# Turning the exponentials of one key block on VectorE and by DMA instead of on TensorE

## The chip, the cores and the metric

The kernel runs on one core of one Trainium2 chip. The metric is the device time of one execution in microseconds (us): the median of three runs of the kernel before was 794.5 us (793.51 to 794.91). Engines are named as the profile names them: PE is TensorE (PEld its weight loads), DVE is VectorE, ACT is ScalarE, POOL is GpSimd, SP is SyncE, which here only issues DMA transfers.

## The reference, cut to what matters

```python
# q, k, v: (8 batches, 8 heads, 576 tokens, 64);  f: (8, 8, 576)
scores = scale * q @ k.T                       # 576 x 576 for each head
cum    = cumsum(log(clip(f, 1e-4, 1)))
scores = where(causal, -1e9, scores + cum[:, :, :, None] - cum[:, :, None, :])
attn   = softmax(scores)
x      = (attn @ v) as (8, 576, 512)
h = relu(x @ w_in); u, v = halves of h         # 512 -> 1024
v_n = layernorm(v); v_s = w_spatial @ v_n + b_spatial
out = (u * v_s) @ w_out
```

## The kernel before, in words

The 64 heads are worked on as 32 **pairs** P of two heads h, four pairs to a batch (`PPB` = 4). The 576 tokens of a head are four query blocks i of 128 and a tail of 64; keys come in the same blocks c. For a pair, `scores(P)` makes q k^T on PE for each query block i and the keys 0 to 128(i+1)-1 (L322), in two pieces: blocks 0, 1, 2 and then block 3. DVE adds the decay and takes the row minimum of the negated scores (L302), ACT takes the exponential and its row sum (L333), DVE forms 1/sum (L348, L349), and POOL scales the rows by it (`share`, L310; for pairs 5 to 7 ACT does, L308). The result lies in `tt[h]` with queries on the partitions. The product with v needs keys on the partitions, so `transposes(P, h)` (L421) turns it: for each key block c one PE transpose for each query block i >= c (L402), 4 + 3 + 2 + 1 of them, into a PSUM bank `tp`, and one copy from there into the tile `e` (L393), in turn by ACT and DVE. `scores_tail` and `transposes_tail` do the same for the 64 queries of the tail. `attend` (L431) then multiplies the blocks of `e` with v (L440) into two PSUM banks, both heads side by side. ACT rounds the sum to `xh` (L449), DVE forms the rest `xl` (L452), and with that the two banks are free for the next scores. `e` has two buffers, one for even and one for odd pairs.

`moe(b)` is the feed-forward part of batch b, nearly all PE matmuls of one pass (L229), its four stages cut into groups that accumulate in two PSUM banks `ps`; its output tile `o` is copied by ACT (L780) and sent to memory by a transfer that SP issues (L782).

The first four pairs run in `first()`, whose order is fixed as written. After that `attention(b)` and `moe(b)` run interleaved: at each `yield` a step says how much PE time it took, and the loop at the end takes next whatever is behind, by the totals `t_attn` and `t_moe`. In the steady state moe(b) thus runs beside the attention of batch b+1. The order in which the rows then stand on every engine's queue is set by a scheduler that runs over the written program at build time; each engine works its queue in order. For pair P, `attention` writes: transposes(P), scores(P+1), transposes_tail(P), scores_tail(P+1), product(P). SP's queue holds, for each pair, the loads of the decay rows `dk` and `dt` (L248, L250), of `qk_t` (L236) and of `vraw` (L287), and between them the outputs `o`.

Of the kernel before, what the change touches and what calls it, by code (L numbers as in the profile page):

```python
# [22 lines left out]
NB = 4  # L23
TL = 512
DM = 512
TOFF = (0, 128, 384, 768)
HALVES = ((0, 256), (256, 320))
QK = 640 + S
EOFF = (0, 640, 1280, 1088, 576)
# [7 lines left out]
def attn_gmlp_kernel(ctx: ExitStack, tc: tile.TileContext, qk, v, f, w_in, w_sp, b_sp, w_out, out):  # L37
# [34 lines left out]
    def decay_rows():  # L72
        ft = wk.tile([64, S], F32, name="ft", tag="vraw")
        SY.dma_start(out=ft, in_=f)
        yield
        ones = wk.tile([64, S], F32, name="ones", tag="xl", bufs=6)
        V.memset(ones, 1.0)
        cum = wk.tile([64, S], F32, name="cum", tag="xh", bufs=6)
        rt = cst.tile([64, RW], F32, name="rt", tag="e1")
        V.tensor_scalar(out=ft, in0=ft, scalar1=1.0e-4, scalar2=1.0, op0=ALU.max, op1=ALU.min)  # L80
        A.activation(ft, ft, AF.Ln)
        A.activation(lnc[0:1, 2:3], ft[0:1, 0:1], AF.Exp)
        V.tensor_tensor_scan(out=cum, data0=ones, data1=ft, initial=0.0, op0=ALU.mult, op1=ALU.add)
# [94 lines left out]
        load64(w_v[:, r, c, :], dh[:, r, c], dl[:, r, c], raw, w[:], t[:], mark)  # L178


    tt = [cst.tile([128, 1280], F32, name=f"tt{h}") for h in range(2)]
    tl = cst.tile([128, 640], F32, name="tl")
    G.memset(tl[:, S:640], 0.0)
    own = {}
# [86 lines left out]
    def mask(P, part=None):  # L271
# [9 lines left out]
        for p in (slice(0, 64), slice(64, 128)) if part != 0 else ():  # L281
            G.affine_select(out=dt[p, TL:S], in_=dt[p, TL:S], compare_op=ALU.is_ge, fill=-8.0 * BIG, base=0,
                            pattern=[[-1, 64]], channel_multiplier=1)

    def prep_v(P):
# [41 lines left out]
    def weigh(P, i, h, tt, dk, at, nm, sm):  # L327

        ps, c, m = at[i, h]
        n = 128 * (i + 1)  # L330
        t = tt[:, TOFF[i]:TOFF[i] + n]
        freed[m] = lowest(t, ps[:, c:c + n], decay(dk, i), nm)
        last["exp", P, h, i] = A.activation(t, t, AF.Exp, bias=nm, scale=-1.0, accum_out=sm)  # L333

    def scores(P):

        qk_t, dk, _ = tab[P]
        tt, _ = turn(P)
        nm = [wk.tile([128, 4], F32, name="nm", tag="nm", bufs=6) for h in range(2)]
        sm = [wk.tile([128, 4], F32, name="sm", tag="sm", bufs=6) for h in range(2)]  # L340
        for piece in ((0, 1, 2), (3,)):
            at = score_piece(P, qk_t, piece)
            yield 250 + 1.68 * 128 * sum(i + 1 for i in piece)
            for i in reversed(piece):
                for h in range(2):
                    weigh(P, i, h, tt[h], dk[h], at, nm[h][:, i:i + 1], sm[h][:, i:i + 1])
        for h in range(2):
            V.tensor_scalar(out=sm[h], in0=sm[h], scalar1=1.0e-9, scalar2=None, op0=ALU.add)  # L348
            V.reciprocal(sm[h], sm[h])  # L349
            for i in range(NB):  # L350
                n = 128 * (i + 1)
                t = tt[h][:, TOFF[i]:TOFF[i] + n]
                share(P, t, sm[h][:, i:i + 1])
        yield 0

    def scores_tail(P):
# [22 lines left out]
            mm(warm[0], zm[:, 0:128], zm[:, 0:512], True, True)  # L379

    nev = [0]
    es = {}

    def e_tile(P):
        if P not in es:
            es[P] = cst.tile([128, 2, 1600], F32, name="e", tag=f"e{P % 2}")
        return es[P]

    copied = {}

# [5 lines left out]
    def turn_block(P, h, c):  # L396
# [3 lines left out]
        tp = bank(2 + c, False) if P < PPB and c > 1 else PS['t'].tile([128, 512], F32, name="tp")  # L400
        for i in range(c, NB):
            T.transpose(out=tp[:, (i - c) * 128:(i - c + 1) * 128],  # L402
                        in_=tt[h][:, TOFF[i] + 128 * c:TOFF[i] + 128 * c + 128], identity=ident)
# [16 lines left out]

    def transposes(P, h):  # L421
        for c in range(NB):
            turn_block(P, h, c)()
            yield 107 * (NB - c)

    def transposes_tail(P):
        for cs, off, step in TAILS:
# [2 lines left out]

    def attend(P, xh, xl):  # L431

        vt, e = vts[P], es.pop(P)
        xb = 4 if P < PPB else 0
        x0, x1 = bank(xb), bank(xb + 1)
        jobs = []
# [1 line left out]
        def product(x, s0, q0, q1, c, h, end):  # L438
            e0 = EOFF[c] - 128 * c
            return lambda: T.matmul(x[64 * h:64 * h + 64, q0 - s0:q1 - s0], vt[:, c, h, :],  # L440
                                    e[:, h, e0 + q0:e0 + q1], start=c == 0, stop=c == end)

        for c in range(NB + 1):
            for x, s0, q0, q1, end in ((x1, 256, max(256, 128 * c), S, NB), (x0, 0, 128 * c, 256, 1)):
                jobs += [product(x, s0, q0, q1, c, h, end) for h in range(2) if c <= end]
        in_one_piece(jobs, copied.pop(P))
        yield 2950
        for ps, s0, n in ((x0, 0, 256), (x1, 256, 320)):
# [16 lines left out]
    def first(ws):  # L465
# [22 lines left out]
        def period(P):  # L488
# [14 lines left out]

            def spread(i, s_, by_a=False):
                for h in range(2):
                    t = tt[h][:, TOFF[i]:TOFF[i] + 128 * (i + 1)]
                    share(PPB + 1 if by_a else 0, t, s_[:, h, 0:1])

            def turned(h):
# [345 lines left out]
```

## Time and profile before

| | |
|---|---|
| median of three runs | 794.5 us |
| the profiled execution, its own time | 796.76 us |
| its span, first to last instruction | 794.8 us |
| PE busy | 759.3 us (96%) |
| DVE, ACT, POOL busy | 436.1 (55%), 418.9 (53%), 368.9 us (46%) |
| granted clock, mean | 0.990 |

All stage times below are on the profiled execution's span, which is 2.0 us shorter than that execution's own time; that time in turn is 2.3 us above the median of the three runs. A busy share is an average over the stages: the views by stretch say which engine is full where.

### The profile page before, as it was taken

The numbers are of one execution on the slowest core, as the hardware profiler recorded it, in microseconds if no ns is written. First come the engines' busy times: TensorE is split into PE (matmuls) and PEld (weight loads), VectorE is DVE, ScalarE is ACT, GpSimd is POOL, SyncE is SP. The second block draws the span as 40 slices with busy tenths as digits, with TensorE's granted clock in tenths as the row PEclk, the third lists the DMA queues.
The fourth block names the chain that finished last, engine by engine and source line by source line (L and its number), as shares of the span: only waits on it lengthen the run. The fifth ranks groups of instructions, "written<-read, shape, count | busy, mean of one in ns | idle before, by whom it ended". The sixth has DMA issues, their size and how long they took to land.

```text
span 794.8 us, 14578 instructions
## 1 busy us (share of the span) xinstructions
PE 759.3 (96%) x4924; PEld 604.5 (76%) x4925; DVE 436.1 (55%) x1509; ACT 418.9 (53%) x1134; POOL 368.9 (46%) x682
## 2 busy tenths in 40 slices
PE   8777898799999999999999999999999999999997
PEld 4445676587887778887788878877788877888896
DVE  6886998645644455444654446445654546543322
ACT  7855587745554456544654446454664446543331
POOL 3976664425544344453732456443544436432231
PEclk9999999899999999999999999999999999999999
DMA  7855254213333213343222243323132342200001
GB/s 218 233 169 160 73 147 155 67 58 123 97 97 123 89 51 95 98 123 122 82 96 67 74 137 97 96 101 103 62 87 89 123 135 81 66 30 31 28 1 67
DMA packets 34316, 78.48 MB, mean 99 GB/s; under 512 B 4161, under 2 KB 8257, under 8 KB 34242
## 3 DMA queue, kind: packets, MB, share of 16 engines
q1 hardware_dynamic: 33922, 77.03, 31.3%
q8 instruction: 39, 0.64, 0.3%
q10 hardware_dynamic: 320, 0.52, 0.2%
q14 instruction: 35, 0.29, 0.1%
HBM read 67.78 MB, written 9.75 MB: 98 GB/s over the span
## 4 chain that ended last, share of the span: by engine, by line
PE 70%; issue 5%; ACT 2%; DMA 2%; POOL 2%; DVE 1%; POOLq 0%; ACTq 0%; DVEq 0%; SPq 0%
PE ps L229 39%; PE sc L440 9%; PE tp L402 8%; PE sc L322 7%; PE sc L229 5%; PE tp L229 2%; DMA out_dram<-o 1%; POOL gl L756 1%; ACT tt L333 1%; PE tp L412 1%; POOL tt L310 1%; DMA dt<-rows_d 1%; DVE tt L302 1%; ACT gh L755 1%; ACT tt L308 0%
## 5 line engine op out<-in xcount | busy, mean ns | idle before, releaser
L333 ACT ACTIVATE tt<-tt,nm 128x128 f32<-128x128 f32 (+2 forms) x240 | 133.7, 558 | 101.5 <-DVE nm L302 99.7
L310 POOL TENSOR_SCALAR tt<-tt,sm 128x128 f32<-128x128 f32 x192 | 100.2, 541 | 109.8 <-DVE sm L349 109.7
L756 POOL TENSOR_TENSOR gl<-u,gh 128x256 fp32r<-128x256 f32 (+1 forms) x64 | 51.5, 806 | 142.4 <-ACT gh L755 141.7
L402 PE MATMUL tp<-ident,tt 128*128 128x128 f32 x588 | 109.4, 283 | 7.8 <-DVE e L393 4.5
L402 PEld LDWEIGHTS tp<-ident,tt 128*128 128x128 f32 x588 | 73.4, 141 | 44.8 <-issue 10.9
L440 PE MATMUL sc<-e,vraw 128*64 128x320 f32 (+4 forms) x896 | 96.8, 368 | 5.8 <-ACT tl L578 4.6
L302 DVE CUSTOM_DVE_ANT_1 tt<-sc,dk 128x256 f32<-128x256 f32 (+1 forms) x120 | 65.8, 552 | 57.5 <-PE sc L322 45.6
L440 PEld LDWEIGHTS sc<-e,vraw 128*64 128x64 f32 x896 | 61.9, 140 | 42.7 <-issue 11.0
L322 PE MATMUL sc<-qk_t 64*128 64x128 f32 (+3 forms) x512 | 87.7, 462 | 3.1 <-DVE nm L302 2.1
L393 DVE COPY e<-tp 128x384 f32<-128x384 f32 (+2 forms) x156 | 69.8, 450 | 26.2 <-PE tp L402 17.9
L393 ACT COPY e<-tp 128x256 f32<-128x256 f32 (+1 forms) x148 | 67.9, 459 | 27.5 <-PE tp L402 24.4
L229 PE MATMUL ps<-sph,vnh 128*128 128x256 f32 (+1 forms) x240 | 75.7, 315 | 1.0 <-DVE u L752 0.7
L229 PE MATMUL ps<-xh,winh 128*128 128x256 f32 (+1 forms) x232 | 74.5, 321 | 1.0 <-DVE vx L701 0.6
L229 PE MATMUL ps<-spl,vnh 128*128 128x256 f32 (+1 forms) x240 | 71.3, 297 | 0.0
L229 PE MATMUL ps<-sph,vnl 128*128 128x256 f32 (+1 forms) x240 | 71.1, 296 | 0.0
L229 PE MATMUL ps<-xh,winl 128*128 128x256 f32 (+1 forms) x232 | 70.8, 305 | 0.0
L229 PE MATMUL ps<-xl,winh 128*128 128x256 f32 (+1 forms) x232 | 69.3, 299 | 0.0
L452 DVE TENSOR_TENSOR xl<-sc,xh 128x256 fp32r<-128x256 f32 x64 | 28.3, 454 | 74.2 <-ACT xh L449 74.2
L322 PEld LDWEIGHTS sc<-qk_t 64*128 64x128 f32 x512 | 44.9, 189 | 26.9 <-issue 9.9
L229 PE MATMUL ps<-winh,xh 128*128 128x512 f32 x148 | 62.1, 420 | 0.7 <-ACT o L780 0.4
L302 DVE CUSTOM_DVE_ANT_0 tt<-sc,dk 128x128 f32<-128x128 f32 (+1 forms) x120 | 49.9, 419 | 20.3 <-PE sc L322 14.9
L229 PE MATMUL ps<-winl,xh 128*128 128x512 f32 x148 | 57.9, 392 | 0.0
(213 smaller groups left out, 1729.7 us busy)
## 6 DMA issues: line engine op xcount, KB each, us to landing
qk_t<-in_dram SPq DMA_DIRECT2D x32, 608.0 KB, 5.5
dk<-rows_d SPq DMA_DIRECT2D x58, 320.0 KB, 4.3
vraw<-in_dram SPq DMA_DIRECT2D x32, 320.0 KB, 3.1
dt<-rows_d SPq DMA_DIRECT2D x58, 144.0 KB, 4.1
out_dram<-o SPq DMA_DIRECT2D x32, 256.0 KB, 2.1
w<-in_dram SPq DMA_DIRECT2D x16, 256.0 KB, 2.8
w<-in_dram SPq DMA_DIRECT2D x4, 512.0 KB, 6.4
d<-rows_d SPq DMA_DIRECT2D x4, 320.0 KB, 6.3
```

Of the source, the lines that this page charges most:

```text
L229: T.matmul(o, l, r, start=st, stop=sp)
L302: return V.tensor_tensor_reduce(out=out, in0=ps, in1=dec, scale=-0.125, scalar=3.0e38, op0=ALU.add, op1=ALU.min, accum_out=acc_)
L310: G.tensor_scalar(out=t, in0=t, scalar1=r, scalar2=1.0, op0=ALU.mult, op1=ALU.mult)
L322: return lambda: T.matmul(ps[:, c:c + n], qk_t[p, n - 128:n], qk_t[p, 640:640 + n], start=True, stop=True)
L333: last["exp", P, h, i] = A.activation(t, t, AF.Exp, bias=nm, scale=-1.0, accum_out=sm)
L393: copied.setdefault(P, []).append(by(out, ps))
L402: T.transpose(out=tp[:, (i - c) * 128:(i - c + 1) * 128], in_=tt[h][:, TOFF[i] + 128 * c:TOFF[i] + 128 * c + 128], identity=ident)
L412: T.transpose(out=tp[:, j * 128:(j + 1) * 128], in_=tl[:, c * 128:(c + 1) * 128], identity=ident)
L440: return lambda: T.matmul(x[64 * h:64 * h + 64, q0 - s0:q1 - s0], vt[:, c, h, :], e[:, h, e0 + q0:e0 + q1], start=c == 0, stop=c == end)
L452: freed[xb + s0 // 256] = V.tensor_tensor(out=xl[:, s0:s0 + n], in0=ps[:, 0:n], in1=f32(xh[:, s0:s0 + n]), op=ALU.subtract)
L755: A.copy(gh[j][:, 0:nt], g)
L756: G.tensor_tensor(out=gl[j][:, 0:nt], in0=g, in1=f32(gh[j][:, 0:nt]), op=ALU.subtract)
```

## The change

From the fifth pair on (P >= 4) key block 0 (`MOVED = (0,)`) is no longer turned by PE. `move(P)` runs at the end of `scores(P)`: for each head DVE turns the four 128x128 pieces of `tt` for keys 0 to 127 in blocks of 32x32 into a tile `mid0`, one instruction of 128 x 512 elements for each head. A turned block lies on the partitions of its queries' group of 32, not of its keys', so 16 DMA transfers within SBUF (4 groups of queries by 4 groups of keys, each 32 partitions x 2 heads x 128 elements of 4 bytes, 32 KB) bring them to the partitions of the keys. They go out on SP's queue. Columns then lie in an order of their own, which `spread` undoes in the product: its matmul reads runs of 64 and writes runs of 32 columns. The 64 tail columns of key block 0 no longer follow on the others, and get a matmul of their own.

So that both fit, `e` has one buffer in place of two, for all pairs; key block 0 of odd pairs goes to a tile `ea`. `tt` gets a stride of 384 columns between query blocks (`ROFF`). `t_attn` is 33600 in place of 37000.

```diff
+RSTEP = 384
+ROFF = tuple(RSTEP * i for i in range(4))
+MOVED = (0,)
...
-        rt = cst.tile([64, RW], F32, name="rt", tag="e1")
+        rt = cst.tile([64, RW], F32, name="rt", tag="mid0")
...
-    tt = [cst.tile([128, 1280], F32, name=f"tt{h}") for h in range(2)]
+    tt = [cst.tile([128, 3 * RSTEP + TL], F32, name=f"tt{h}") for h in range(2)]
...
                 share(P, t, sm[h][:, i:i + 1])
+        move(P)
         yield 0
...
-    es = {}
+    e_all = cst.tile([128, 2, 1600], F32, name="e", tag="e")
     def e_tile(P):
-        if P not in es:
-            es[P] = cst.tile([128, 2, 1600], F32, name="e", tag=f"e{P % 2}")
-        return es[P]
+        return e_all
+    def e_first(P):
+        return aside[P] if P in aside else e_all
...
     def transposes(P, h):
         for c in range(NB):
-            turn_block(P, h, c)()
-            yield 107 * (NB - c)
+            if c not in MOVED:
+                turn_block(P, h, c)()
+                yield 107 * (NB - c)
+    def move(P):
+        tt, _ = turn(P)
+        for c in MOVED:
+            w = 128 - 32 * c
+            mid = cst.tile([128, 2, 4, w], F32, name=f"mid{c}", tag=f"mid{c}")
+            for h in range(2):
+                V.transpose(out=part(mid[:, h], 0, [[32, NB - c], [w, 4], [1, 32]]),
+                            in_=part(tt[h][:, ROFF[c] + 128 * c:], 0, [[RSTEP, NB - c], [32, 4], [1, 32]]))
+            if P % 2:
+                aside[P] = cst.tile([128, 2, 512], F32, name="ea")
+            e = e_first(P)
+            for g in range(4):
+                for r in range(4):
+                    copied.setdefault(P, []).append(SY.dma_start(
+                        out=e[32 * r:32 * r + 32, :, EOFF[c] + w * g:EOFF[c] + w * g + w],
+                        in_=mid[32 * g:32 * g + 32, :, r, :]))
...
+        def spread(x, m0, c, h, end):
+            k0 = max(m0, c)
+            n, w = m0 + 2 - k0, 128 - 32 * c
+            src = part(e_first(P)[:, h, EOFF[c] + 32 * (k0 - c):], 0, [[w, 4], [32, n], [1, 32]])
+            out = part(x[64 * h:64 * h + 64, 128 * (k0 - m0):], 0, [[32, 4], [128, n], [1, 32]])
+            return lambda: T.matmul(out, vt[:, c, h, :], src, start=c == 0, stop=c == end)
...
+            if P == PPB:
+                move(P)
             for h in range(2):
                 yield from transposes(P, h)
...
-    t_attn, t_moe = 37000.0, 52500.0
+    t_attn, t_moe = 33600.0, 52500.0
```

**PE, at the product of the fifteenth pair (P = 14)**, which in the trace of before starts at 345.84 us. `sc` are PSUM banks, `tp` the banks of transposes, `ps` those of moe; line 440 is the product, 322 the scores of the next pair but one. Before:

```order
L440 MATMUL sc_4228<-e_4035,vraw_4001 64x320 x2
L440 MATMUL sc_4227<-e_4035,vraw_4001 64x256 x2
...
L440 MATMUL sc_4228<-e_4035,vraw_4001 64x64 x2
L402 MATMUL tp_4318<-ident_63,tt0_82 128x128
L229 MATMUL ps_4274<-sph_78,vnh_3500 128x320
...
L402 MATMUL tp_4328<-ident_63,tt0_82 128x128 x3
...
L402 MATMUL tp_4346<-ident_63,tt0_82 128x128 x2
...
L322 MATMUL sc_4399<-qk_t_4291 128x384
```

The same place on PE in the changed kernel, where lines 483 and 475 are the product, 413 the transposes and 328 the scores; tile `e_88` is now the one buffer of `e`:

```order
L483 MATMUL sc_4333<-e_88,vraw_4102 64x4x2x32 x2
L475 MATMUL sc_4333<-e_88,vraw_4102 64x64 x2
L483 MATMUL sc_4332<-e_88,vraw_4102 64x4x2x32 x2
...
L475 MATMUL sc_4333<-e_88,vraw_4102 64x64 x2
L232 MATMUL ps_4252<-woh_76,gh_4248 128x512
...
L232 MATMUL ps_4321<-woh_76,gl_4249 128x512
L413 MATMUL tp_4436<-ident_63,tt0_82 128x128 x2
L413 MATMUL tp_4442<-ident_63,tt0_82 128x128
L328 MATMUL sc_4480<-qk_t_4401 128x384
```

The first product of 320 columns is now one of 256 and one of 64; the run of four transposes of key block 0 is gone; and between the product's end and the next scores there stand 6 matmuls of moe of 512 columns and 3 transposes, where before there were 28 of 320 columns and 6 transposes.

**DVE, from the scores of pair 15 to the product of pair 14.** `sm` are the row sums and their inverses, `u` is moe's, `tl` the tail, `xl` the rest behind the product. In the changed kernel:

```order
L355 RECIPROCAL sm_4189<-sm_4189 128x4
L803 TENSOR_TENSOR u_4065<-ps_4216,u_4065 128x256
L449 STREAM_TRANSPOSE mid0_4275<-tt0_82 128x4x4x32
L404 COPY e_88<-tp_4299 128x3x2x64
L308 ISA tl_84,nm_4307<-sc_4309,dt_4108 128x288
...
L375 TENSOR_TENSOR nm_4307<-nm_4307 128x1
L449 STREAM_TRANSPOSE mid0_4275<-tt1_83 128x4x4x32
L377 TENSOR_SCALAR sm_4308<-sm_4308 128x1
...
L501 TENSOR_TENSOR xl_4331<-sc_4332,xh_4330 128x256
```

The two new instructions stand ahead of the copy of the tail into `e`, on which the product waits, and ahead of `xl`, on which the next scores wait.

**SP, the loads around pairs 14 and 15** (`o` is an output of moe). Before:

```order
L250 DMA dt_4007<-rows_d_73 64x576 x2
L287 DMA vraw_4001<-in_1_dram 128x640
L248 DMA dk_4293<-rows_d_73 128x640
L236 DMA qk_t_4540<-in_0_dram 128x1216
L248 DMA dk_4294<-rows_d_73 128x640
L782 DMA out_dram<-o_4207 128x512
L250 DMA dt_4295<-rows_d_73 64x576 x2
L782 DMA out_dram<-o_4249 128x512
```

In the changed kernel:

```order
L253 DMA dt_4405<-rows_d_73 64x576 x2
L456 DMA ea_4278<-mid0_4275 32x2x128 x16
L833 DMA out_dram<-o_4318 128x512
L293 DMA vraw_4399<-in_1_dram 128x640
L833 DMA out_dram<-o_4359 128x512
L251 DMA dk_4660<-rows_d_73 128x640
L239 DMA qk_t_4952<-in_0_dram 128x1216
L251 DMA dk_4661<-rows_d_73 128x640
```

The sixteen transfers of a pair stand behind its `dt` and ahead of an output, of `vraw` for the pair's product and of the next `dk`; they cannot go out before both turns on DVE are done.

## Rows read from the trace of the kernel before

**Rows 1.** The page: busy time of the engines over the span.

```profile
PE 759.3 (96%) x4924; PEld 604.5 (76%) x4925; DVE 436.1 (55%) x1509; ACT 418.9 (53%) x1134; POOL 368.9 (46%) x682
```

**Rows 2.** Busy time by stretch: the middle of the span, in which pairs 8 to 31 run beside moe. Columns: stretch, its length, busy us (and instructions) of PE, PEld, DVE, ACT, POOL, granted clock, DMA share, GB/s.

```profile
200.00:720.00 520.00, 518.40 (x3455) 418.98 (x3454) 269.14 (x979) 270.66 (x742) 239.00 (x462) 1.00 0.30 93
```

**Rows 3.** The same view of the stretch in which pairs 4 and 5 run beside the first part of moe(0) and the loading of its weights.

```profile
90.00:130.00 40.00, 35.76 (x235) 27.95 (x233) 38.01 (x109) 31.27 (x87) 24.45 (x36) 1.00 0.39 117
```

**Rows 4.** The page: the chain of work that ended last, share of the span by engine.

```profile
PE 70%; issue 5%; ACT 2%; DMA 2%; POOL 2%; DVE 1%; POOLq 0%; ACTq 0%; DVEq 0%; SPq 0%
```

**Rows 5.** PE in order of time, a run of four transposes and what follows it. Columns: start us, us to the end of the last, line, operation, tiles, count.

```profile
356.02 0.60 PE L402 MATMUL tp<-ident,tt 128*128 128x128 f32 x4
356.37 0.39 PE L229 MATMUL ps<-sph,vnl 128*128 128x320 f32 x1
356.60 0.31 PE L229 MATMUL ps<-sph,vnh 128*128 128x320 f32 x1
356.75 0.31 PE L229 MATMUL ps<-spl,vnh 128*128 128x320 f32 x1
```

**Rows 6.** Busy time by stretch of the transposes of line 402 alone: PE, PEld.

```profile
300.00:400.00 100.00, 16.70 (x89) 11.13 (x90) 1.00 0.33 102
```

**Rows 7.** The product of pair 15 on PE with a run of transposes and the matmul after it, in order of time; and its matmuls by shape (between 200 and 700 us: count, busy us, mean ns of one).

```profile
369.70 2.92 PE L440 MATMUL sc<-e,vraw 128*64 128x320 f32 x28
372.55 0.66 PE L402 MATMUL tp<-ident,tt 128*128 128x128 f32 x4
372.97 0.47 PE L229 MATMUL ps<-winh,xh 128*128 128x512 f32 x1
...
L440 PE MATMUL sc<-e,vraw 128*64 128x320 f32 x264 | 47.9, 441 | 0.0
L440 PE MATMUL sc<-e,vraw 128*64 128x256 f32 x88 | 13.2, 379 | 0.0
```

**Rows 8.** Copies and other DVE and ACT instructions by shape, same stretch and columns.

```profile
L393 DVE COPY e<-tp 128x384 f32<-128x384 f32 x65 | 35.8, 551 | 9.9 <-PE tp L402 5.6 <-PE tp L412 4.0
L302 DVE CUSTOM_DVE_ANT_1 tt<-sc,dk 128x512 f32<-128x512 f32 x44 | 30.1, 684 | 38.2 <-PE sc L322 38.2
L393 ACT COPY e<-tp 128x512 f32<-128x512 f32 x43 | 25.0, 583 | 2.7 <-PE tp L402 2.2
L393 DVE COPY e<-tp 128x128 f32<-128x128 f32 x43 | 12.2, 283 | 4.8 <-PE tp L402 4.6
```

**Rows 9.** From the last scores of pair 15 to the product of pair 14, in order of time on PE, DVE and POOL: the scores of query block 3, the second inverse, the copy of the tail, the scaling of head 0 (x4), a mask, the scaling of head 1 (x4), the product.

```profile
339.26 1.13 PE L322 MATMUL sc<-qk_t 64*128 64x512 f32 x4
343.37 0.18 DVE L349 RECIPROCAL sm<-sm 128x4 f32<-128x4 f32 x1
343.47 0.53 DVE L393 COPY e<-tp 128x384 f32<-128x384 f32 x1
...
342.49 2.07 POOL L310 TENSOR_SCALAR tt<-tt,sm 128x128 f32<-128x128 f32 x4 [3.41 <-DVE sm L349]
345.61 0.41 POOL L276 TENSOR_SCALAR_AFFINE_SELECT dk<-dk 128x256 f32<-128x256 f32 x1 [1.05 <-DMA dk<-rows_d]
346.36 2.06 POOL L310 TENSOR_SCALAR tt<-tt,sm 128x128 f32<-128x128 f32 x4
...
345.84 2.93 PE L440 MATMUL sc<-e,vraw 128*64 128x320 f32 x28
```

**Rows 10.** SP: transfers in order of time (start, us of issue); the issue of `dt` (ns, least, median, most) and its landing; the landing of the outputs; and the queue over the whole span (packets, MB, share of 16 engines).

```profile
341.19 0.33 SPq L248 DMA_DIRECT2D dk<-rows_d  x1
341.57 0.42 SPq L236 DMA_DIRECT2D qk_t<-in_dram  x1
342.10 0.37 SPq L248 DMA_DIRECT2D dk<-rows_d  x1
L250 SPq DMA_DIRECT2D dt<-rows_d x58: 450/468/625, 18.8 to 692.5; - x58
DMA to landing us min/median/max: 3.0/4.3/7.6
DMA to landing us min/median/max: 2.0/2.3/6.7
q1 hardware_dynamic: 33922, 77.03, 31.3%
```

**Rows 11.** Behind two products, on ACT and DVE in order of time: a copy into `e` and the two halves of `xh` on ACT, the last half of `xl` on DVE, for the product of pair 17, which ends at 417.23 us; then an output copy that waits for a transfer, `xh` and `xl` for the product of pair 14, which ends at 348.77 us.

```profile
414.35 0.59 ACT L393 COPY e<-tp 128x512 f32<-128x512 f32 x1 [0.44 <-PE tp L402]
417.28 0.43 ACT L449 CAST xh<-sc 128x320 fp32r<-128x320 f32 x1 [0.60 <-PE sc L440]
417.74 0.49 DVE L452 TENSOR_TENSOR xl<-sc,xh 128x320 fp32r<-128x320 f32 x1 [0.61 <-ACT xh L449]
...
350.07 0.59 ACT L780 COPY o<-ps 128x512 f32<-128x512 f32 x1 [3.20 <-DMA out_dram<-o]
350.55 0.71 ACT L449 CAST xh<-sc 128x256 fp32r<-128x256 f32 x2
350.96 0.82 DVE L452 TENSOR_TENSOR xl<-sc,xh 128x256 fp32r<-128x256 f32 x2 [3.73 <-ACT xh L449]
```

More of the change, by code (lines that the diff above doesn't have):

```diff
@@ L283, in mask, with off @@
                             pattern=[[-1, 64]], channel_multiplier=1)
+    def off(P):
+        return ROFF if P >= PPB else TOFF
     def prep_v(P):
@@ L330, in weigh @@
         n = 128 * (i + 1)
-        t = tt[:, TOFF[i]:TOFF[i] + n]
+        t = tt[:, off(P)[i]:off(P)[i] + n]
         freed[m] = lowest(t, ps[:, c:c + n], decay(dk, i), nm)
@@ L351, in scores @@
                 n = 128 * (i + 1)
-                t = tt[h][:, TOFF[i]:TOFF[i] + n]
+                t = tt[h][:, off(P)[i]:off(P)[i] + n]
                 share(P, t, sm[h][:, i:i + 1])
+        move(P)
         yield 0
@@ L381, in attn_gmlp_kernel @@
     nev = [0]
-    es = {}
+    e_all = cst.tile([128, 2, 1600], F32, name="e", tag="e")
     def e_tile(P):
-        if P not in es:
-            es[P] = cst.tile([128, 2, 1600], F32, name="e", tag=f"e{P % 2}")
-        return es[P]
+        return e_all
+    def e_first(P):
+        return aside[P] if P in aside else e_all
+    aside = {}
     copied = {}
@@ L402, in turn_block @@
             T.transpose(out=tp[:, (i - c) * 128:(i - c + 1) * 128],
-                        in_=tt[h][:, TOFF[i] + 128 * c:TOFF[i] + 128 * c + 128], identity=ident)
+                        in_=tt[h][:, off(P)[i] + 128 * c:off(P)[i] + 128 * c + 128], identity=ident)
         return lambda by=None: evac(P, e_tile(P)[:, h, EOFF[c]:EOFF[c] + n], tp[:, 0:n], by)
@@ L422, in transposes, with part @@
         for c in range(NB):
-            turn_block(P, h, c)()
-            yield 107 * (NB - c)
+            if c not in MOVED:
+                turn_block(P, h, c)()
+                yield 107 * (NB - c)
+    def part(t, k, steps):
+        return bass.AP(tensor=t.tensor, offset=t.offset, ap=[list(t.ap[0]), *steps])
+    def move(P):
[14 more added lines that the diff above has]
+                        in_=mid[32 * g:32 * g + 32, :, r, :]))
     def transposes_tail(P):
@@ L431, in attend @@
     def attend(P, xh, xl):
-        vt, e = vts[P], es.pop(P)
+        vt, e = vts[P], e_tile(P)
+        moved = MOVED if P >= PPB else ()
         xb = 4 if P < PPB else 0
@@ L440, in product @@
             return lambda: T.matmul(x[64 * h:64 * h + 64, q0 - s0:q1 - s0], vt[:, c, h, :],
-                                    e[:, h, e0 + q0:e0 + q1], start=c == 0, stop=c == end)
+                                    e[:, h, e0 + q0:e0 + q1], start=c == 0 and c not in moved, stop=c == end)
+        def spread(x, m0, c, h, end):
[4 more added lines that the diff above has]
+            return lambda: T.matmul(out, vt[:, c, h, :], src, start=c == 0, stop=c == end)
         for c in range(NB + 1):
             for x, s0, q0, q1, end in ((x1, 256, max(256, 128 * c), S, NB), (x0, 0, 128 * c, 256, 1)):
-                jobs += [product(x, s0, q0, q1, c, h, end) for h in range(2) if c <= end]
+                if c > end:
+                    continue
+                if c in moved:
+                    jobs += [spread(x, s0 // 128, c, h, end) for h in range(2)]
+                    if end < NB:
+                        continue
+                    q0 = TL
+                jobs += [product(x, s0, q0, q1, c, h, end) for h in range(2)]
         in_one_piece(jobs, copied.pop(P))
@@ L505, in spread @@
                 for h in range(2):
-                    t = tt[h][:, TOFF[i]:TOFF[i] + 128 * (i + 1)]
+                    t = tt[h][:, off(X)[i]:off(X)[i] + 128 * (i + 1)]
                     share(PPB + 1 if by_a else 0, t, s_[:, h, 0:1])
```

## Prediction

> **What bounds the kernel now.** I read the page's first parts, then the busy times by stretch, then the chain, then single pairs in order of time. PE is busy for 96% of the span [rows 1]. By stretch that is two cases: from 200 to 720 us PE is busy 518.4 of 520 us at the full granted clock, while DVE, ACT and POOL stand near one half [rows 2], and two products in a row start 23.9 us apart [rows 7, 9]; between 90 and 130 us, where pairs 4 and 5 run while weights are still converted, DVE is busy 95% and PE 89% [rows 3]. The chain agrees: 70% of it is PE [rows 4]. So in the steady state, which holds 24 of the 28 changed pairs (8 to 31), PE time taken away is time won, as long as nothing new makes PE wait; in the early part it is not.
>
> **What PE loses.** Per pair 8 transposes go (4 for each head). Their price is not the duration of one in the trace, since they overlap: a run of four starts 0.35 us ahead of the next instruction, and that one is followed after 0.23 us where 0.15 is usual [rows 5], so the run costs 0.35 + 0.08 = 0.43 us; another starts 0.42 us ahead of its successor [rows 7]. That is 0.108 each. By their busy time, 16.70 us for 89, each would cost 0.188 [rows 6]; that counts the tail that lies under the next matmul and is the upper bound. I take 0.108, since the next start is what moves: 8 x 0.108 = 0.86 us a pair. [...]
>
> **What PE gains.** The product of key block 0 has the same columns as before, cut as 256 + 64 + 256 for each head where it was 320 + 256: four more instructions of 64 columns (the trace has each of these matmuls as two) among 28 that take 2.85 us from their first start to the next instruction [rows 7]. Lower bound 0, since columns are unchanged; upper bound four times the mean, 4 x 0.102 = 0.41 us. Rows of 320 and 256 columns differ by 62 ns in the mean, so time goes by columns, and I take 0.05. Whether reading runs of 64 and writing runs of 32 columns costs anything no row shows; I take nothing. At half speed the 512 columns would cost their share of 1,600, 2.85 x 512 / 1600 = 0.91 us a pair, and eat the gain. Net: 0.86 - 0.05 = 0.81 us a pair, 24 x 0.81 = 19.4 us in the steady state.
>
> **What is added elsewhere.** DVE gets two instructions of 128 x 512 a pair. Nearest rows: 0.28 us for a copy of 128 columns, 0.55 for 384, 0.68 for another operation of 512 [rows 8]; bounds 0.55 and twice 0.68, I take 0.65. The copies from PSUM go on alternating, eight in place of ten, by which DVE gives up a 384 and a 128 and takes a 256 instead (about 0.45 us); so DVE gets 0.85 us more a pair, ACT about 0.9 less. With half of DVE free this is hidden in the steady state. In the early part it is not: two pairs there cost 2 x 0.85 = 1.7 us, and the other two early pairs, where PE is fuller, give back 2 x 0.81. I count the four as nothing.
>
> **The new waits.** DVE now waits for POOL. For pair 15: the scores end at 340.4, the second inverse at 343.55, POOL has scaled head 0 at 344.56 and, after a mask that waits for its load, head 1 at 348.42 [rows 9]. The first turn thus ends near 345.2, the copy of the tail behind it near 345.75 where it was done at 344.0, and the product needs it at 345.84, that is 5.3 us after the scores' end. Counted in the built order with the distance of starts from [rows 5] (0.15 us for 320 columns and in proportion for others, 0.108 for a transpose), PE has 6.4 to 9.5 us of other work at this place for pairs 9 to 30, where before it had 4.7 to 6.4. So it is covered; without the cover it would be about 0.6 us a pair. Behind the second turn (349.1) stand the tail's inverse and `xl`, and `xl` waits for the product anyway.
>
> SP then issues the 16 transfers. An issue takes 0.33 us for `dk`, 0.47 in the median for `dt` and 0.63 at most [rows 10]: 5.3 to 10 us for sixteen. The last lands 2.3 to 4.3 us later, by the medians of outputs and of loads, so at 357 to 363.5. The product of that pair starts near 369 (369.7 before, less 0.8): 5.5 us or more of slack. `vraw` behind them goes out near 360 at the latest and lands near 364, for the same product. The output behind them delays the next output copy on ACT, but the built order has ten rows of ACT between the two copies. Traffic: 448 x 64 pieces of 512 bytes are 14.7 MB. By bytes that adds 6% to the 31% of [rows 10], by pieces at the queue's mean (0.117 us each) 26%; neither fills the engines.
>
> The last is the single buffer of `e`. Copies into `e` for pair P+1 must now wait until the product of P has read it, and stand ahead of `xh` on ACT; before, such a copy ran under the product [rows 11]. After the product PE needs `xl` done for the next scores: 1.0 us behind the product when nothing interferes, 3.0 when ACT waits for an output first [rows 11]. A copy of 0.55 us in front makes it 1.0 to 1.55. PE's other work at this place was 3.4 to 6.3 us before; in the built order it is 1.7 us for about five pairs, 2.2 for eight, over 3.5 for the rest. So the cover is nearly gone. I put 2 us in all on it and on other small waits.
>
> **The sum.** 796.8 (the profiled execution) - 19.4 + 0 + 2 = 779.4 us. The median of the runs shown is 2.3 us below the profiled execution, so 777.0 us for the median, 2.2% less. What this measurement can tell from no change is about 0.2%, 1.6 us.
>
> **Rivals.**
> *The waits eat most of it.* If `xl` comes 3.0 us behind the product as in the worse row of [rows 11], five pairs lose 1.3 us and eight lose 0.8, 13 us in all: 788. For it: the cover shrank to 1.7. Against: the 3.0 came from an output copy ahead of `xh`, which now stands behind it. 0.13.
> *No change.* The strided product at half speed, or DVE's turns at twice 0.68 us with the waits above: within 0.2% of 794.5. Against: unit runs of 64 and 32 columns. 0.05.
> *Slower: the transfers come too late.* The product of each pair then waits for them. That starts when sixteen issues and one landing outlast the 19.8 us from the second turn (349.1) to the product near 368.9: (19.8 - 4.3) / 16 = 0.97 us an issue. A product that is x late holds back the scores two pairs on, since those of the next pair stand ahead of it on PE, so every second pair pays x; the gain is gone when x is 1.6 us, at 1.07 us an issue. At 1.2 us x is 3.7, 12 x 3.7 = 44 us, and the time 821. For it: sixteen transfers in a row, each from SBUF to SBUF, are nowhere in the trace, and SP holds the next pair's loads behind them. Against: the longest issue of `dt` is 0.63 us. [...] 0.09.
> *More is won.* All 28 pairs gain, and a transpose is worth 0.14 us, between the two prices above: 28 x 8 x 0.14 = 31 us, 763. For it: the runs that go also held PSUM banks, and I count no gain in the early part. Against: DVE there. 0.07.
> My forecast holds the rest, 0.66, with its own range 769 to 785.
>
> **How the numbers follow.** Faster by over 0.2%: 0.66 + 0.13 + 0.07 = 0.86; within: 0.05; slower: 0.09. For eight in ten I take the forecast's range and reach up to the case of the waits and down towards the better one: 766 to 789. It leaves out the slower case, no change, and what is beyond.
>
> **What the profile after should show.** Transposes of tt on PE at 12 a pair in the steady state and about 10 us of their busy time in 100 us where it was 16.7 [rows 6]; PE still over 99% busy there, with a pair's period shorter by 0.8 us; the two turns near 0.65 us each, the second waiting 1 to 2 us for POOL; the 16 issues within 10 us of one another and landed 5 us or more before the product. The forecast is wrong if the product waits for a transfer, if scores wait for `xl` in most pairs, if the product takes more than 3.1 us, or if pairs 4 to 7 take several us longer than before.

## The result, and the profile after

The changed kernel is slower: 804.7 us in the median (803.8 to 806.4) beside 794.7 us of the kernel before on the same chip, a ratio of 1.0122 with a 95% interval of 1.0087 to 1.0156. The forecast was 777.0 us, with a range of 766 to 789. The profiled execution of after took 804.2 us, with a span of 802.4.

The page of after: busy time; SP's DMA queue (packets, MB, share of 16 engines); the chain by engine and by line; and the issues of the new transfers (count, KB each, median us to landing).

```profile
PE 741.0 (92%) x4812; PEld 589.2 (73%) x4813; DVE 466.6 (58%) x1537; ACT 395.3 (49%) x1106; POOL 369.1 (46%) x682
...
q1 hardware_dynamic: 69762, 91.74, 38.9%
...
PE 46%; SPq 10%; POOL 9%; DVE 6%; issue 5%; DMA 5%; ACT 4%; POOLq 0%; ACTq 0%; DVEq 0%
PE ps L232 28%; SPq L456 10%; POOL tt L316 6%; PE sc L328 5%; PE sc L232 4%; DMA out_dram<-o 3%; PE sc L475 3%; PE tp L413 2%; PE tp L232 2%; PE sc L483 2%; DVE tt L308 1%; DVE vx L758 1%; DVE mid L449 1%; DMA dk<-rows_d 1%; PE tp L423 1%
...
e<-mid SPq DMA_DIRECT2D x224, 32.0 KB, 1.9
```

PE is busy 18.3 us less than in [rows 1], so the work did leave it. But its idle time (span less busy) went from 35.5 to 61.4 us, and the span grew by the difference, 7.6 us. The chain says where to look: in [rows 4] it was 70% PE with 0% for SP's queue; now it is 46% PE, and 10% is the queue issuing the transfers of line 456.

Busy time by stretch in the steady state, to be read beside [rows 2]; and three short stretches around one gap (PE, PEld, DVE, ACT, POOL, granted clock, DMA share, GB/s):

```profile
200.00:720.00 520.00, 496.79 (x3278) 400.93 (x3278) 292.25 (x977) 246.13 (x704) 233.92 (x449) 0.98 0.38 111
...
455.00:465.00 10.00, 10.00 (x72) 7.57 (x68) 4.81 (x20) 4.63 (x14) 3.25 (x6) 1.00 0.21 53
465.00:470.00 5.00, 0.39 (x2) 0.00 (x0) 1.09 (x5) 0.62 (x2) 0.00 (x0) 0.76 0.49 142
470.00:474.00 4.00, 3.98 (x9) 3.14 (x10) 0.00 (x0) 2.30 (x8) 0.24 (x1) 0.50 0.32 114
```

In the steady state PE now stands idle for 23 of 520 us, where it was 1.6. This gap costs twice: behind the idle time from 465.4 to 470.0 us PE works at 0.50 of its clock, 9 matmuls in 4 us. Over the span the mean clock falls from 0.990 to 0.979; by it 7.9 and 16.9 us of full speed are missing.

The chain in order of time around that gap (start, us, what):

```profile
432.00 0.71 DVE mid L449
...
432.96 0.42 SPq L456
...
444.22 2.20 DMA out_dram<-o
446.50 0.59 ACT o L831
447.09 0.36 ACT gh L806
447.52 0.89 POOL gl L807
...
452.80 2.04 POOL tt L316 x4
454.86 0.71 DVE mid L449
...
467.11 2.20 DMA out_dram<-o
469.38 0.59 ACT o L831
470.02 5.08 PE ps L232 x12
```

This is a loop, and it goes through a queue that does no work. POOL's scaling releases the second turn on DVE, the turn releases 16 issues on SP, behind which an output stands. Only when that output has landed is the one tile `o` free for ACT's next copy. Behind that copy wait, on ACT's queue, moe's `gh`, from there POOL's `gl`, and behind `gl` POOL's scaling of the next pair, which starts the loop again; or PE waits for the PSUM bank that the copy empties.

SP's issues in the same stretch (start, us of issue, transfers in a row):

```profile
432.74 11.38 SPq L456 DMA_DIRECT2D ea<-mid  x16
444.22 0.53 SPq L833 DMA_DIRECT2D out_dram<-o  x1
...
453.59 0.50 SPq L253 DMA_DIRECT2D dt<-rows_d  x1
455.60 11.41 SPq L456 DMA_DIRECT2D e<-mid  x16
467.11 0.53 SPq L833 DMA_DIRECT2D out_dram<-o  x1
...
468.16 0.50 SPq L253 DMA_DIRECT2D dt<-rows_d  x1
```

The sixteen hold the queue for 11.4 us. Twice in a row an output follows them at once. The second time the loads of `dt` are split: one half goes at 453.59, the other at 468.16, behind the sixteen. The waits of the steady state (200 to 720 us: us in total, times, longest) show both effects, first in after, then in the kernel before:

```profile
POOL dt L285 <- DMA dt<-rows_d: 72.7, 24, 13.0
ACT o L831 <- DMA out_dram<-o: 37.4, 13, 6.4
PE ps L232 <- ACT o L831: 14.7, 5, 4.6
```

```profile
ACT o L780 <- DMA out_dram<-o: 34.6, 14, 3.4
POOL dt L282 <- DMA dt<-rows_d: 0.7, 3, 0.3
```

ACT waited for outputs before too, and nearly as long in total, but at most 3.4 us at a time, and no matmul of PE waited for ACT's copy in this stretch; now the longest is 6.4 us, and five times PE stands still behind it, 14.7 us in all. POOL's mask of `dt` waits 72.7 us where it waited 0.7.

### The profile page after: what moved, and what is told of

It is laid out like the page before. It is cut to its first block, busy times and chain, and to the rows that moved or that the text cites. A ratio compares the mean times of both kernels' runs of the same rounds, so it can differ in the third digit from the quotient of the medians.

```text
span 802.4 us, 15003 instructions
## 1 busy us (share of the span) xinstructions
PE 741.0 (92%) x4812; PEld 589.2 (73%) x4813; DVE 466.6 (58%) x1537; ACT 395.3 (49%) x1106; POOL 369.1 (46%) x682
## 4 chain that ended last, share of the span: by engine, by line
PE 46%; SPq 10%; POOL 9%; DVE 6%; issue 5%; DMA 5%; ACT 4%; POOLq 0%; ACTq 0%; DVEq 0%
PE ps L232 28%; SPq L456 10%; POOL tt L316 6%; PE sc L328 5%; PE sc L232 4%; DMA out_dram<-o 3%; PE sc L475 3%; PE tp L413 2%; PE tp L232 2%; PE sc L483 2%; DVE tt L308 1%; DVE vx L758 1%; DVE mid L449 1%; DMA dk<-rows_d 1%; PE tp L423 1%
## 5 line engine op out<-in xcount | busy, mean ns | idle before, releaser
L339 ACT ACTIVATE tt<-tt,nm 128x384 f32<-128x384 f32 (+1 forms) x240 | 133.4, 558 | 58.8 <-DVE nm L308 56.7
L475 PEld LDWEIGHTS sc<-e,vraw 128*64 128x64 f32 x784 | 55.6, 138 | 32.4 <-issue 5.7
L475 PE MATMUL sc<-e,vraw 128*64 128x320 f32 (+4 forms) x784 | 73.3, 324 | 5.5 <-ACT tl L627 4.3
L404 ACT COPY e<-tp 128x384 f32<-128x384 f32 (+2 forms) x120 | 45.6, 380 | 55.0 <-PE tp L413 24.7
L413 PE MATMUL tp<-ident,tt 128*128 128x128 f32 x364 | 67.4, 280 | 5.2 <-ACT e L404 3.1
L404 DVE COPY e<-tp 128x384 f32<-128x384 f32 (+2 forms) x128 | 57.9, 455 | 22.9 <-PE tp L413 20.6
L413 PEld LDWEIGHTS tp<-ident,tt 128*128 128x128 f32 x364 | 46.0, 142 | 25.2 <-issue 4.8
L449 DVE STREAM_TRANSPOSE mid<-tt 128x512 f32<-128x512 f32 x56 | 39.7, 708 | 37.0 <-POOL tt L316 31.1
L232 PE MATMUL ps<-winl,xh 128*128 128x512 f32 x148 | 60.3, 408 | 0.0
L308 DVE CUSTOM_DVE_ANT_0 tt<-sc,dk 128x384 f32<-128x384 f32 (+1 forms) x120 | 49.7, 418 | 10.6 <-PE sc L328 9.6
```

Of the source, the lines that this page charges most:

```text
L232: T.matmul(o, l, r, start=st, stop=sp)
L308: return V.tensor_tensor_reduce(out=out, in0=ps, in1=dec, scale=-0.125, scalar=3.0e38, op0=ALU.add, op1=ALU.min, accum_out=acc_)
L404: copied.setdefault(P, []).append(by(out, ps))
L413: T.transpose(out=tp[:, (i - c) * 128:(i - c + 1) * 128], in_=tt[h][:, off(P)[i] + 128 * c:off(P)[i] + 128 * c + 128], identity=ident)
L449: V.transpose(out=part(mid[:, h], 0, [[32, NB - c], [w, 4], [1, 32]]), in_=part(tt[h][:, ROFF[c] + 128 * c:], 0, [[RSTEP, NB - c], [32, 4] ...
```

## The experiments

Theory A: SP's queue, held by the sixteen issues, makes what stands behind them late, the outputs above all. Rivals: B, the single buffer of `e`; C, DVE's turns and their wait for POOL; later D, the traffic of the pieces on the DMA engines; and the built order by itself.

**Outputs on ACT's queue, all else as in after.**

```diff
-            (SY if p0 == 0 else A).dma_start(out=out[bb, tok:tok + np_, :], ...)
+            A.dma_start(out=out[bb, tok:tok + np_, :], ...)
```

> The changed kernel with one line altered: every output tile is sent from ACT's own queue, right behind the copy that made it, and no longer from SP's queue behind the sixteen transfers. Theory A (SP's queue: sixteen issues of 0.64 us each, 10.3 us, hold back the output, the output's landing holds back ACT's next output copy, and PE waits for the PSUM bank under it): the 15 to 17 us that PE waits for that copy go, and the slower clock behind the waits too; 779 to 790 us. Theory B (the single buffer of e took the cover away) and theory C (VectorE stands still ahead of its turns while GpSimd scales): nothing changes, 801 to 807.

782.4 us (781.2 to 784.5), ratio 0.9828 [0.9805, 0.9851]: this one edit takes away 22 us. The chain, the steady stretch and two waits of this kernel:

```profile
PE 69%; POOL 5%; DVE 4%; DMA 3%; issue 2%; ACT 1%; SPq 0%; POOLq 0%; DVEq 0%; ACTq 0%
```

```profile
200.00:720.00 520.00, 511.21 (x3427) 416.32 (x3427) 301.52 (x995) 255.28 (x716) 237.87 (x453) 1.00 0.40 114
```

```profile
POOL dt L285 <- DMA dt<-rows_d: 13.4, 19, 2.6
ACT o L831 <- DMA out_dram<-o: 2.5, 4, 0.8
```

SP's queue is gone from the chain, and PE is idle for 8.8 us in this stretch where it was 23; no matmul waits for ACT's output copy any more. The transfers, their number and their bytes are the same. The scheduler builds a new order with this edit too (on PE the two traces differ from the 1421st of 4812 instructions on), so this pair of runs alone can't part the queue from the order; the other built orders below bear on that.

**The same without the change**, on the kernel before:

> The kernel before with all its outputs on ACT's queue in place of SP's. Theory A: SP's queue is free when an output comes, so nothing is won: 793 to 797 us. Rival: outputs on SP were a cost of their own, and the 22 us between the changed kernel and the one with its outputs on ACT say nothing of the sixteen issues: 775 to 786 us.

800.9 us, ratio 1.0059 [1.0032, 1.0085]. Outputs on ACT's queue are no gain of their own; before the change they cost 5 us, more than A had said. So the 22 us go with the sixteen issues ahead of the outputs.

**One buffer of `e`, nothing moved.**

```diff
-MOVED = (0,)
+MOVED = ()
...
-    t_attn, t_moe = 33600.0, 52500.0
+    t_attn, t_moe = 37000.0, 52500.0
```

> The changed kernel with no key block moved: TensorE turns all of them as before, with the new stride of tt, the old pace of 37000 and the single buffer of e. It shows the price of the single buffer alone. The changed kernel took 804.7 us where its shorter TensorE work would give 777, so 28 us are to be found. Theory B: most of them are here, 815 to 822 us. Theories A and C: as the kernel before, 793 to 798.

796.6 us, ratio 1.0005 [0.9991, 1.0018]. B falls: with all transposes on PE the single buffer costs nothing, and in the changed kernel itself scores waited for `xl` only three times between 200 and 720 us, 3.4 us in all.

**The turns alone**: PE makes all transposes and the product reads them; DVE's two turns a pair go into `mid0`, which nothing reads; no transfers, `t_attn` 37000.

```diff
-            if c not in MOVED:
-                turn_block(P, h, c)()
+            turn_block(P, h, c)()
...
-        moved = MOVED if P >= PPB else ()
+        moved = ()
...
```

> As the kernel with one buffer and all transposes on TensorE, and from the fifth pair on VectorE makes its two turns of 128 x 512 for each pair as in the changed kernel, with nobody reading them and no transfers. It shows the price of the turns and of their waiting for GpSimd. Theory C: 18 to 28 us above the kernel with one buffer. Theories A and B: 0 to 4 us above it.

798.5 us, ratio 1.0022 [1.0004, 1.0040]: 56 turns cost some 2 us in all, where C asked for 18 to 28. C falls.

**Turns and transfers**: the same with the sixteen transfers a pair into a tile that nothing reads.

```diff
+            ea = cst.tile([128, 2, 512], F32, name="ea")
+            for g in range(4):
+                for r in range(4):
+                    SY.dma_start(out=ea[32 * r:32 * r + 32, ...], in_=mid[32 * g:32 * g + 32, :, r, :])
```

> As the kernel with the turns only, and behind them the sixteen transfers of each pair on SP's queue, into a tile that nobody reads; TensorE still turns everything itself and the product does not wait for the transfers. It shows the price of the transfers' place in SP's queue. Theory A: 18 to 30 us above the kernel with the turns only. Theories B and C: 0 to 3 us above it.

806.8 us, ratio 1.0122 [1.0090, 1.0154], 8 us above the turns alone where A asked for 18 to 30. The starts of two products tell where: pair 12's stands at 310.2 us in this trace and at 302.5 with the turns alone, 7.7 us apart; pair 31's at 748.2 and 740.4, 7.8 apart. So all of it is lost before pair 12 and nothing after, though the transfers go on. The built order differs: here most outputs stand on SP's queue ahead of a pair's sixteen,

```profile
473.12 0.34 SPq L829 DMA_DIRECT2D out_dram<-o  x1
473.59 11.66 SPq L453 DMA_DIRECT2D ea<-mid  x16
```

and not behind them. To see whether the early 8 us are outputs too, the same kernel with its outputs on ACT's queue:

> The kernel with turns and sixteen unread transfers a pair beside all transposes (806.8 us), its outputs on ACT's queue in place of SP's. Its transfers do no useful work. Theory A: its 8 us above the kernel with turns alone (798.5) are outputs and sixteen transfers in each other's way, so most of them go: 797 to 802. If those 8 us come from the early part for another reason (traffic beside the weights' loading): 803 to 808.

811.3 us, ratio 1.0184 [1.0169, 1.0199]: A's expectation fails, and the time is above the other range too. Pair 12's product starts at 308.3 us, still 5.8 later than with the turns alone; the 5.3 us more that are lost from there to pair 31 are about what outputs on ACT's queue cost the kernel before. So the early loss is not the outputs. In the stretch 140 to 180 us (turns alone, then turns and transfers) PE does less, at a lower clock, while the DMA engines are twice as busy.

```profile
140.00:180.00 40.00, 37.16 (x221) 28.68 (x223) 25.16 (x93) 25.66 (x72) 14.77 (x25) 0.96 0.28 84
```

```profile
140.00:180.00 40.00, 33.29 (x181) 21.70 (x182) 32.62 (x104) 25.50 (x74) 20.65 (x37) 0.83 0.54 154
```

By busy time and granted clock, an estimate, PE did 35.7 and 27.6 us of full-speed work there: 8 us less, the whole early loss. What stands on SP's queue just before this stretch differs: the last loads of moe's weights (`w`), with turns alone and then with the transfers:

```profile
132.42 0.38 SPq L125 DMA_DIRECT2D w<-in_dram  x1
```

```profile
135.29 10.80 SPq L453 DMA_DIRECT2D ea<-mid  x16
146.20 2.85 SPq L125 DMA_DIRECT2D w<-in_dram  x3
```

With the transfers three of these loads go out only behind a pair's sixteen, and POOL's last instruction of the weights' conversion starts at 167.9 us where it was 148.2 (166.6 with the outputs on ACT's queue). So the traces point to the same blocked queue, with weights behind the sixteen in place of outputs; no run moved the weights' loads, so this is not shown, and the doubled traffic is not ruled out.

**Plain transfers**: the same sixteen, each 32 partitions x 1 KB in one run, outputs on SP. Key block 0 goes to tiles of its own, `ea0` and `ea1`, for even pairs too.

```diff
+            e = aside[P] = cst.tile([128, 4, 2 * w], F32, name="ea", tag=f"ea{P % 2}")
...
-                        out=e[32 * r:32 * r + 32, :, EOFF[c] + w * g:EOFF[c] + w * g + w],
-                        in_=mid[32 * g:32 * g + 32, :, r, :]))
+                        out=e[32 * r:32 * r + 32, g, :], in_=mid[32 * g:32 * g + 32, r, :]))
```

> The changed kernel with the same 16 transfers a pair on SP's queue and the outputs still behind them, but each transfer plain: 32 partitions x 1 KB in one run on both sides (both heads side by side in `mid0` and in the target tile) where it was 32 x 2 x 128 elements. Theory A (SP's queue is held by the issues, and the output behind them is late): if the time of an issue goes by the number of pieces, it falls from 0.595 us to 0.35 to 0.45, sixteen take 6 to 7 us in place of 10.3, and the kernel lands between the changed one and the one with its outputs on ACT's queue: 785 to 796 us. If the time of an issue does not depend on the shape (still 0.55 to 0.6), A gives 800 to 806, no change. A rival, D: what costs is the pieces' traffic on the DMA engines (448 x 64 pieces of 512 bytes), not the issues; then half the pieces give 790 to 797 even at an unchanged issue.

807.3 us, ratio 1.0134 [1.0093, 1.0175]. The issue row (least, median, most, ns) and the queue:

```profile
L454 SPq DMA_DIRECT2D ea<-mid x448: 507/589/1667, 77.2 to 726.9; - x150
```

```profile
q1 hardware_dynamic: 55426, 91.74, 38.5%
```

Half the pieces are gone (14,336 packets fewer), an issue still takes 0.589 us, and the kernel's time did not fall; it is 1 us above what A gave for an unchanged issue, within the scatter of its runs (802.0 to 810.2). D falls. With plain transfers and the outputs on ACT's queue:

> The plain transfers of 32 x 1 KB and all outputs on ACT's queue. If nothing but the outputs suffered from the held queue: 781 to 784 us, as with the 2-piece transfers. If the loads behind the sixteen (`vraw`, `dk`, `dt`) still lose something and the issues get shorter: 775 to 780.

781.5 us, ratio 0.9821 [0.9805, 0.9837], the same as with transfers of two pieces.

**A second buffer for `o`**, outputs on SP. The weights' loads use the same buffers before the first output, so their tile gets a second one too.

```diff
-        raw = mo.tile([128, 2, 128, 2], U32, name="w64", tag=("gt0", "gt1", "o")[n % 3], bufs=1)
+        raw = mo.tile([128, 2, 128, 2], U32, name="w64", tag=("gt0", "gt1", "o")[n % 3], bufs=(1, 1, 2)[n % 3])
...
-        tag, bufs = ("vx", 2) if b == B - 1 and nps[0] % 3 else ("o", 1)
+        tag, bufs = ("vx", 2) if b == B - 1 and nps[0] % 3 else ("o", 2)
```

> The changed kernel with two buffers for moe's output tile `o` where it has one; the outputs stay on SP's queue behind the sixteen transfers. Theory A says the loop runs: sixteen issues, output issued late, its landing, then ACT's next copy into the only `o`, then PE's bank. With a second buffer that copy no longer waits for the transfer just ahead of it, and the loop is cut at another place than by another queue: 782 to 792 us, and the waits of ACT for the output's landing fall from 45.7 us to under 15. If it is not the output but the loads behind the sixteen (masks on POOL wait 81 us for `dt`) or the traffic that costs, nothing changes: 800 to 808.

795.3 us, ratio 1.0001 [0.9979, 1.0022], above the 782 to 792 that A gave. ACT's wait for outputs falls from 37.4 to 8.6 us (200 to 720), as A said, but only 9 of the 22 us come back, so A was too narrow. The chain of this kernel shows the other half:

```profile
463.34 2.22 DMA out_dram<-o
465.63 0.60 ACT o L831
466.25 0.53 SPq L833
466.88 0.78 SPq L251
...
468.86 0.49 SPq L253
469.40 8.13 DMA dt<-rows_d
```

An output at the head of SP's queue waits there for ACT's copy, and the next pair's loads `dk` and `dt` wait behind it. Late outputs and late loads are two ends of one blocked queue; the other queue for outputs frees both.

**Five issues in place of sixteen**: one transfer writes `mid0` to DRAM, four read it back, outputs on SP. The tiles `ea0` and `ea1` are as with the plain transfers.

```diff
+            md = dr.tile([128, 4 * 2 * w], F32, name="md")
+            SY.dma_start(out=md[:], in_=mid)
+            mv = md[:].rearrange("(g k) (r x) -> r k g x", g=4, r=4)
+            for r in range(4):
+                ... SY.dma_start(out=e[32 * r:32 * r + 32, :, :], in_=mv[r])
```

> The changed kernel with another way for the turned block: one transfer writes all of `mid0` to DRAM, four read it back onto the partitions of the keys; five issues on SP's queue a pair in place of sixteen, the outputs still behind them, and twice the bytes. The reads wait on the queue for the write, about 0.5 + 2.2 us, so the queue is held some 5 us in place of 10.3. Theory A: most of the loss is gone, 781 to 792. If the bytes or the pieces cost and not the time for which the queue is held: 800 to 815.

789.9 us, ratio 0.9930 [0.9908, 0.9951]. Its SP rows:

```profile
429.26 0.33 SPq L453 DMA_DIRECT2D md<-mid  x1
432.81 1.75 SPq L456 DMA_DIRECT2D ea<-md  x4
```

The queue is held for 5.3 us, the wait for the write with it, in place of 11.4, and 15 of the 22 us come back, although the bytes of the queue rise from 91.7 to 106.4 MB. So it is the time for which the queue is held that goes with the loss. With the outputs on ACT's queue besides:

> The five transfers through DRAM and all outputs on ACT's queue. Theory A: nothing is left to be won by a shorter hold when no output stands behind it, 778 to 784, within 3 us of the sixteen transfers with outputs on ACT's queue (781.5 and 782.4). If loads behind the sixteen still cost there: 773 to 778. If the bytes cost: over 785.

782.5 us, ratio 0.9843 [0.9794, 0.9893]: where no output stands behind them, five issues and sixteen come out the same, within this run's 4 us either way.

**The early pairs**: outputs on ACT's queue, key block 0 moved from P = 9 on.

```diff
-            if c not in MOVED:
+            if c not in MOVED or P < 2 * PPB + 1:
...
-        moved = MOVED if P >= PPB else ()
+        moved = MOVED if P > 2 * PPB else ()
...
```

> Outputs on ACT's queue (782.4 us), key block 0 moved only from the tenth pair on (P = 9); pairs 4 to 8 turn it on PE as before. If those five gain as the later ones (0.8 to 1.0 us each), the kernel comes to 786 to 788; if they lose, 776 to 781; if they come out even, 781 to 784.

786.2 us, ratio 0.9891 [0.9856, 0.9925]. Leaving five early pairs on PE costs 3.8 us by the medians, 0.75 each, and 5 us by the ratios; the two intervals together leave room for about 2 to 8. So the early pairs gain, and the size fits that of the others.

The same kernel moved from the ninth pair on (P = 8) took 798.6 us, but it computes something else and says nothing of the early pairs: pair 8's transfers write key block 0 into the one `e` before pair 7's product has read its own block there, and that product waits 7.3 us for them. The tenth pair's block goes to `ea`, where this can't happen.

**Other built orders**: `t_attn` 37000, then 35000, outputs on SP, nothing else changed.

```diff
-    t_attn, t_moe = 33600.0, 52500.0
+    t_attn, t_moe = 37000.0, 52500.0
```

> The changed kernel with t_attn 37000 in place of 33600, outputs on SP as they were. In its built order of SP, per batch, one output stands right behind a sixteen and two stand behind the next pair's sixteen and `vraw`; in the changed kernel it is two sixteens in a row with an output right behind each, and loads behind outputs. If the loss is set by these places, fewer outputs right behind a sixteen lose less: 785 to 798. If any output behind a sixteen costs the same wherever it stands: 800 to 808.

> The changed kernel with t_attn 35000. Per batch of its built order of SP, as with 37000 one output stands right behind a sixteen and two behind the next sixteen and `vraw`, but in the early part (pairs 9 to 12) outputs stand between the transfers of one pair, where they hold back the rest of that pair's sixteen. Places theory: 790 to 802, above the one with 37000. If places do not matter: 800 to 808.

803.3 us, ratio 1.0075 [1.0050, 1.0101], and 795.9 us, ratio 0.9987 [0.9970, 1.0003]. The first missed its 785 to 798; the second met its range, but not its place above the first. The order is worth up to 9 us here, but my reading of which places cost was too coarse to rank the orders. With 37000 POOL waits only 9.5 us for `dt` (200 to 720), ACT still 38.4 us for outputs and PE 11.5 us for ACT's copy: the late `dt` alone is not the loss. With the outputs on ACT's queue in these two orders:

> t_attn 35000 and outputs on ACT's queue. Theory A (outputs behind the sixteen on SP cost, in each built order): 780 to 786 where the same total with outputs on SP took 795.9. If the order and not the outputs makes the difference: 792 to 797.

> t_attn 37000 and outputs on ACT's queue. Theory A: 780 to 788 where the same total with outputs on SP took 803.3. If the order and not the outputs makes the difference: 798 to 804.

777.8 us, ratio 0.9771 [0.9742, 0.9799], and 778.7 us, ratio 0.9786 [0.9768, 0.9804], both under the ranges given. In three built orders the outputs' queue is worth 22, 18 and 25 us, so the gain is no luck of one order. The kernel with 35000 has the lowest time of this study, 2.3% under the kernel before; PE is busy for 513.95 us of its steady stretch of 520.

## Why the prediction was wrong, step by step

- **What bounds the kernel: right.** Where the queue is freed the chain is PE again, and PE's work sets the time.
- **PE's term: right in kind, a little small.** PE's transposes of line 413 from 300 to 400 us are busy for 10.21 us, where "about 10" was forecast and [rows 6] had 16.70. Busy time less what the clock withheld fell from 759.3 - 7.9 = 751.4 to 741.0 - 16.9 = 724.1 us; the withheld time is taken as lying all in busy time, so this is rough. 27 us over 28 pairs are 0.97 a pair, where I had 0.81 over 24. Counting the early four as nothing was probably too careful, as the run with five early pairs left on PE showed.

```profile
300.00:400.00 100.00, 10.21 (x56) 6.95 (x55) 0.98 0.38 115
```

- **The strided product: right.** Its matmuls of 256 columns take 392 ns in the mean, 379 in [rows 7], 13 ns for each of eight a pair, and from pair 5 on the whole product takes 2.94 us where it took 2.92 to 2.93. **The turns: right**, 0.71 us where 0.65 was taken, and the wait for POOL ahead of the second is 28.2 us over 26 times, 1.1 each, where "1 to 2" was forecast.

```profile
L449 DVE STREAM_TRANSPOSE mid<-tt 128x512 f32<-128x512 f32 x42 | 29.8, 710 | 33.3 <-POOL tt L316 27.6 <-DMA dk<-rows_d 5.5
L483 PE MATMUL sc<-ea,vraw 128*64 128x256 f32 x88 | 13.2, 392 | 0.0
```

- **The sixteen issues: too short.** 0.595 us and a gap of 0.04 make 10.3 us when nothing interferes and 11.4 around 440 us, beyond the upper bound of 10 that came from the longest issue of `dt` [rows 10]. The landing, 1.9 us, was shorter than assumed. The product never waits for them: those issued until 444.1 belong to a product that starts at 454.6. The slower rival, transfers too late for the product, therefore did not happen at 0.64 us an issue, as its own threshold of 0.97 said; the kernel became slower by another path. So its chance of 0.09 for a slower kernel covered the sign, not the mechanism. The queue's share of the DMA engines rose by 7.6 points, near the 6 forecast by bytes.
- **The step that failed** is one sentence: "The output behind them delays the next output copy on ACT, but the built order has ten rows of ACT between the two copies." I had the mechanism and waved it off by counting rows where time was wanted. In the trace two such copies stand at 458.69 and 469.38 us on ACT. The seven rows between them are done at 462.94, and the second copy has waited 6.45 us, because the output of the first, ready at 459.3, is issued only behind the sixteen, at 467.11. And what waits behind that copy was not followed further: ACT's `gh`, POOL's `gl`, POOL's scaling, the next turn. I looked at the transfers' own reader, the product, and found 5 us of slack; the readers of what stands behind them had none.

```profile
458.69 0.59 ACT L831 COPY o<-ps 128x512 f32<-128x512 f32 x1 [0.71 <-ACT xh L498]
...
469.38 0.58 ACT L831 COPY o<-ps 128x512 f32<-128x512 f32 x1 [6.45 <-DMA out_dram<-o]
```

- **The loads behind the outputs** were not in the sum. I asked only when `vraw` goes out, not what an output waiting at the head of the queue does to `dk` and `dt`: POOL's mask waits 72 us more. What that wait costs by itself no run shows.
- **The 2 us for small waits.** The single buffer was rightly cheap (0.0 within 0.2%). With the outputs on ACT's queue and the forecast's own `t_attn` of 33600 the kernel needs 782.4 us, with 35000 777.8: without the failed step the sum, 777.0, is met within 5 us, or 1. That the second is so near is partly luck: it is the best of three orders, and not the one forecast.
- **The signs.** None of the four by which I wanted to know that the forecast was wrong came: no product waited for one of the sixteen transfers, scores seldom waited for `xl`, the product stayed under 3.1 us (but for pair 4's, 4.0 us), and the products of pairs 4 to 7 start at 103.6 to 169.1 us where it was 108.5 to 184.0. All four look at the moved work and its own readers. Of what the profile was to show, PE over 99% busy failed: 496.79 of 520 us are 95.5%.

The issue time of the sixteen was the loss: sixteen times 0.64 us, and 18 to 25 us came back when outputs left that queue. Five issues in place of sixteen gave back 15 us, by the time for which the queue is held (5.3 us in place of 11.4) and not by the bytes, which rose from 91.7 to 106.4 MB.

What stays open: whether the sixteen transfers beside all transposes cost their 6 to 8 us before pair 12 by the weights' loads behind them, as the traces suggest, and which place of an output among them costs how much. The first would need those loads on another queue, the second the orders changed one row at a time; neither was tried.

## What to carry to other kernels

Treat a queue that only issues transfers as an engine: count what a new burst of issues holds it for, and then follow every row behind the burst to its reader, not only the burst's own reader. Slack is counted in microseconds, never in rows. Where such a queue closed the loop, taking the unrelated rows off it gave back most (22 us), fewer issues less (15), and a second buffer, which cuts only one link, least (9).

## What the runs showed of the hardware

An issue's time on SP did not go by bytes or pieces. From SBUF to SBUF over 32 partitions it is 0.595 us for 64 pieces of 512 bytes and 0.589 for 32 of 1 KB; 512 KB from SBUF to DRAM over 128 partitions issue in 0.326 us, 128 KB back over 32 partitions in 0.423. These are the rows of the kernel that goes through DRAM (least, median, most, ns):

```profile
L453 SPq DMA_DIRECT2D md<-mid x28: 325/326/458, 76.2 to 706.0; - x28
...
L456 SPq DMA_DIRECT2D ea<-md x112: 303/423/1860, 79.9 to 710.7; - x112
```

And in the changed kernel PE paid again after standing idle: at 1.00 up to 465 us, without a matmul for 4.6 us from 465.4 on, its granted clock then stood at 0.50 until 474 us.
